# Where the end of an attention layer splits its output weights, and where it turns two projected tiles

## The chip, the cores and the metric

The kernel runs on one core of a Trainium2 chip. A core has a matrix engine (TensorE, PE in the profile, with its weight loads as PEld), a vector engine (VectorE, DVE), an activation engine (ScalarE, ACT), a general one (GpSimd, POOL) and a queue engine (SyncE, SP) that issues most transfers here. Each engine works through its own list of instructions in order and waits on semaphores for the others. The metric is the device time of one execution, in microseconds. Fewer is better.

## The reference

Four layers in a row on one sequence of 2048 tokens of 576 features, each added to its input: attention, a spectral filter, attention again, the filter again, with the same weights both times.

```python
def _A_ref(x, wqkv, wo):            # H = 32 heads of 18, window W = 256
    qkv = (x @ wqkv).reshape(B, S, 3, H, Dh).transpose(2, 0, 3, 1, 4)
    scores = jnp.einsum("bhqd,bhkd->bhqk", q, k) * (Dh ** -0.5)
    mask = (idx[:, None] - idx[None, :] >= 0) & (idx[:, None] - idx[None, :] < W)
    p = _softmax(jnp.where(mask[None, None], scores, -1e9), axis=-1)
    o = jnp.einsum("bhqk,bhkd->bhqd", p, v)
    return (lambda x, *d: x.transpose(*d))(o, 0, 2, 1, 3).reshape(B, S, D) @ wo

def _B_ref(x, w_r, w_i):
    X = jnp.fft.rfft2(x) * (w_r + 1j * w_i)
    return jnp.fft.irfft2(X, s=(S, D), axes=(-2, -1))

x = A_x
x = x + _A_ref(_layernorm(x), A_wqkv, A_wo)
x = x + _B_ref(_layernorm(x), B_w_r, B_w_i)
x = x + _A_ref(_layernorm(x), A_wqkv, A_wo)
x = x + _B_ref(_layernorm(x), B_w_r, B_w_i)
```

## The kernel before

Matrix products are made in two parts for accuracy: an operand is split into a high part, rounded to the matrix engine's format, and a low part, the rest; three products of parts then stand for one. So every weight and every turned tile goes through a copy (high) and a subtraction (low) before PE can use it.

**The attention's rounds.** `layer_a` treats the 32 heads as 8 groups of 4, and a group's 2048 queries as 16 tiles of 128: 128 rounds, numbered 0 to NX - 1 = 127. In a round PE makes the scores `S` of a query tile (`score_max`, L1155), of which DVE takes the row maximum (L1157), ten rounds ahead of their use. It makes the scores again the other way round, `E`, for one key tile against up to three query tiles (`exps`, L1192): 384 wide, but 256 and 128 for the last two tiles of a group (rounds 110 and 111 are such). ACT takes the exponential of each into `P` (L1193), four to a round, POOL masks the finished `P` (L1195, L1198), and PE multiplies `P` with the values into the bank `U` (`part`, L1212). After four query tiles `U` is copied to `us` (L1217), turned (L1226), copied to `ts` and divided (`norm`), and stored to memory as `o_d`. `m_rows` turns the maxima and puts them, as `mt` (L1170), beside the queries.

Up to round MIX - 1 = 117 `bursts` emits this in steps of three scores of each kind: the step's `E` and exponentials, its `S`, then a few `part`s, then the left work such as `norm`, and last, for each round whose fourth exponential lies in the step, `behind(round)`. From round 118 a plain loop emits the exponentials and products that are left, and calls `behind` at the end of each round. There are three PSUM banks for `E`, three for `S`, one (`pj`) for projections and one for `U`.

**What `behind` lays under the rounds.** It prepares the output projection, class `Out`, with OB = NX - 8 = 120. Round 104: `room` issues two transfers on SP's queue, the raw output weights' first two fifths and then the other three (L720), into the tile `ofree`, which the tile of projected inputs has left. Rounds 110, 112, 114, 116 and 118: `split(0)` to `split(4)`, one fifth each, on ACT (L727) and then POOL (L728), from `ofree` into `oroom`. Rounds 107 to 115: `const` loads the next layer's tables, `dc` (L734). Then the loads of inputs and of `o_d`, and `turn` of tiles 0 to 2 in the bank `pj`.

**The end of the attention.** A tile `u` of 128 tokens is projected in eleven pairs of products that need all but the last head group (`early`) and three pairs for that group (`late`), which ends with two sums on DVE into the tile's input (L809). `turn(u, ...)` makes four transposes on PE (L761, L762) into a bank, a copy of the bank to `oT[u % 3]` on ACT or DVE (L766) and a subtraction on DVE (L770). `tail(u)` is two small operations on POOL. The last group's part is turned by `turn_last` (PE, L775) and split by `split_last` (ACT copy L780, DVE subtraction L781). The last round's `us` is turned in `tpz`, whose fourth bank is `U`, and divided straight into `o7` (L1438 to L1442). After these lines `spectral` starts `layer_b`, which projects the tiles 3 to 15 by `unit`, the first thing it asks of PE, in banks that the attention has left.

Of the kernel before, what the change touches and what calls it, by code (L numbers as in the profile page):

```python
# [850 lines left out]
def layer_a(tc, ident, eps, bp, src, dst, wqk_d, wv_d, wo_d, dc_d, gc_d, dram, copy, wvs, second, spectral, share):  # L851

    nc = tc.nc
    V, A, T, P = nc.vector, nc.scalar, nc.tensor, nc.gpsimd
# [14 lines left out]
    if True:  # L869
# [192 lines left out]
        with ExitStack() as c2:  # L1062
# [233 lines left out]
            def bursts():  # L1296
# [8 lines left out]
                for k in range(-(-len(es) // 3)):  # L1305
# [50 lines left out]
                    for x, pair, hp in e:  # L1356
                        if pair == hp == 1:
                            behind(x)
# [7 lines left out]
            OB = NX - 8  # L1366
            out = Out(nc, ident, eps, bp, ov, o7v, srcv, dstv, wo_d, dc_d, gc_d, second)

            def behind(t):
                if copy and t >= 32 and t % 4 == 0 and t < 32 + 16 * len(copy):  # L1370

                    z, r = divmod(t // 4 - 8, 4)
                    P.dma_start(*[a[32 * r:32 * r + 32] for a in copy[z]])
                if t == OB - 16:
                    out.room()
                if 0 <= t - (OB - 10) < 10 and t % 2 == 0:
                    out.split((t - (OB - 10)) // 2)
                if t - OB + 13 in range(0, 10, 2):
                    out.const((t - OB + 13) // 2)
                if t == OB - 3:  # L1380
                    out.filters()
                if t - OB + 8 in range(0, 10, 2):
                    out.load_x(((t - OB + 8) // 2 + 1) % 5)
                if t - OB in (0, 1, 2):
                    out.load_o(t - OB)
                if t == OB + 3:
                    out.last(slice(96, 128), slice(0, 56))
                if t == NX - 2:
                    out.last(slice(0, 64), slice(0, 128))
                if t == NX - 1:  # L1390
                    out.last(slice(64, 96), slice(0, 128))

                if t - OB - 3 in (0, 1, 2, 5):
                    out.tail(min(t - OB - 3, 3))
                if t - OB - 5 in (0, 1, 2):
                    u = t - OB - 5
                    out.turn(u, pp.tile([128, 512], F32, tag="pj", name=f"tpa{u}", bufs=1), V)
                    out.load_o(u + 3)
                if t == NX:

                    A.activation(wp.tile([128, 1], F32, name="se", bufs=1), eps, AF.Sqrt)
# [4 lines left out]
            U = pp.tile([128, 512], F32, tag="U", name="U", bufs=1)  # L1406
# [5 lines left out]
            for t in range(MIX, NX + 2):  # L1412
                loads(t)
                for pair in range(2):
                    for hp in range(2):
                        if t < NX:
                            exps(t, pair, hp)
                    if pair == 0 and t - 2 < NX:
                        pv(t - 2)

                y = t - 3 if t == NX - 2 else t - 4
                if MIX < y < NX - 1 and y % 4 == 3 and t != NX - 1:
                    due.append((norm, *divmod(y // 4, 4)))
                for f, *a in due[:1]:
                    f(*a, *([True] if f is norm else []))
                    due.pop(0)
                behind(t)
            assert not due
            def bank(tag, name):
                return pp.tile([128, 512], F32, tag=tag, name=name, bufs=1 if tag == "pj" else 3)  # L1430
# [12 lines left out]
                             rc.to_broadcast([32, 4, 4, 18]))  # L1443
            out.early(0, None, slice(4, 11))
            out.early(1, [bank("S", f"ops1_{k}") for k in range(2)])
            out.early(2, [bank("E", f"ops2_{k}") for k in range(2)])
            out.tail(4)
            tp = bank("E", "tpl")
            for u in range(4):
                out.turn_last(u, tp[:, 128 * u:128 * u + 128])  # L1450
            for u in range(3):
                out.split_last(u, tp[:, 128 * u:128 * u + 128])
            out.turn(3, U, A)
            out.late(0)
            out.split_last(3, tp[:, 384:512])
            out.late(1)
            out.turn(4, U, A)
            out.late(2)
            out.turn_last(4, tp[:, 0:128])
            out.split_last(4, tp[:, 0:128])  # L1460
# [4 lines left out]
def prompt_kernel(tc, x, wqk, wv, wo, w, dc, fc, gc, ga, m2, out):  # L1465
    nc = tc.nc
    with ExitStack() as ctx, tc.manual_schedule():
        pool = lambda *a, **k: ctx.enter_context(tc.tile_pool(*a, **k))
        dram = pool(name="dram", bufs=1, space=bass.MemoryType.DRAM)
        t = [dram.tile([S, 2 * NF], F32, name=f"x{i}") for i in range(3)]  # L1470
        cr = {k: dram.tile(list(v.shape), F32R, name=k + "r") for k, v in (("dc", dc), ("gc", gc))}
        wvs = dram.tile([2, 128, 5 * D], F32R, name="wvs")
        wo2 = dram.tile([128, 10 * NF], F32, name="wo2")
        drs = [pool(name=f"dram{i}", bufs=1, space=bass.MemoryType.DRAM) for i in range(2)]
        cp, bp = pool(name="ac", bufs=1), pool(name="abig", bufs=1)
        ident = cp.tile([128, 128], F32, name="ident")
        make_identity(nc, ident)
        eps = cp.tile([128, 1], F32, name="eps"); nc.vector.memset(eps, 1e-5)
        layers, share = [], {}
        for i, (s, a, d) in enumerate(((x, t[0], t[1]), (t[1], t[2], out))):  # L1480
            layers.append(layer_a(tc, ident, eps, bp, s, a, wqk, wv, wo2 if i else wo, cr["dc"], cr["gc"], drs[i],
                                  [(cr[k], v) for k, v in (("dc", dc), ("gc", gc))] if i == 0 else None, wvs, i > 0,
                                  lambda *args, i=i, d=d: layer_b(tc, args[0], d, *args[1:], ga, fc, m2, w, wo, wo2, drs[i], layers[1] if i == 0 else None, share), share))
        for layer in layers:
            for _ in layer:
                pass
# [18 lines left out]
```

## Time and profile before

| | us |
|---|---|
| median of 3 runs (1369.69 to 1375.65) | 1369.79 |
| profiled execution, its time | 1370.11 |
| its span | 1368.4 |
| busy in the span: PE / DVE / ACT / POOL | 1337.2 / 901.1 / 780.3 / 644.1 |
| mean granted clock of PE (1 is full) | 0.997 |
| `E` scores L1192 / exponentials L1193, 1024 each | 222.2 / 409.1 |
| projection products L786, the 812 in `ops` banks | 115.4 |
| split's casts L727, 10 / one | 676 ns median |
| split's subtractions L728, 10 / one | 1423 ns median |

The ends of the two attention layers lie near 420 to 482 us and 1122 to 1183 us. A timeline row gives the start in us, the duration (of a merged row: of all its instructions), the engine, the line, the operation and the tiles as out<-in, the count, and in brackets how long the engine had been idle before and what released it. A row of the waits gives who waited for whom, the total in us, the number of times and the longest. A row of stretches gives, from one time to another, the length, the busy us of PE, PEld, DVE, ACT and POOL with their instructions, the granted clock of PE, the share of the DMA engines' time and GB/s.

### The profile page before, as it was taken

To read this page: it belongs to the slowest core of one execution; us is meant where nothing else is said; L and a number is where in the kernel's file an instruction comes from. 1 tells how busy PE (TensorE), PEld (TensorE's weight loads), DVE (VectorE), ACT (ScalarE), POOL (GpSimd) and SP (SyncE) were. 2 spreads that over 40 slices of the span, in tenths; PEclk is the share of its full clock that TensorE was granted. 3 is DMA by queue.
4 is the path that set the end of the run, shared out by engine and by line. 5 is a ranking of instruction groups with operands and counts; after the bars stand their busy time and mean duration, and the time that the engine had idled before them with its cause. 6 is when DMAs were issued, how large, how long until landed. Compare 5 with 4: busy or idle time off the path is not lost.

```text
span 1368.4 us, 33594 instructions
## 1 busy us (share of the span) xinstructions
PE 1337.2 (98%) x11356; PEld 998.4 (73%) x11356; DVE 901.1 (66%) x3060; ACT 780.3 (57%) x1966; POOL 644.1 (47%) x1152
## 2 busy tenths in 40 slices
PE   9999999999999999998999999999999999998998
PEld 8986666666665699975999965566666655898587
DVE  5418777877778376666673157777777785575855
ACT  5622777777778544542355316677777778463223
POOL 2257554555546533476221394445555458112721
PEclk9999999999999999999999999999999999999999
DMA  6756665655446457677873468556555565597874
GB/s 199 209 166 193 205 188 172 186 165 160 151 145 182 127 158 247 222 240 256 271 230 74 113 194 221 163 171 167 153 152 151 160 161 166 143 362 254 287 252 158
DMA packets 202356, 259.11 MB, mean 189 GB/s; under 512 B 104530, under 2 KB 109906, under 8 KB 201674
## 3 DMA queue, kind: packets, MB, share of 16 engines
q1 hardware_dynamic: 191546, 235.76, 57.2%
q10 hardware_dynamic: 7648, 14.96, 3.1%
q0 software_dynamic: 2992, 6.25, 1.8%
q8 instruction: 92, 1.51, 0.5%
q14 instruction: 78, 0.64, 0.2%
HBM read 156.17 MB, written 101.01 MB: 188 GB/s over the span
## 4 chain that ended last, share of the span: by engine, by line
PE 87%; DMA 4%; DVE 3%; ACT 2%; issue 2%; POOL 1%; SPq 0%; ACTq 0%; DVEq 0%; POOLq 0%
PE pj L1098 18%; PE S L1155 12%; PE U L1212 12%; PE vps L991 8%; PE ops L786 7%; PE E L1192 6%; PE po L257 4%; PE pq L512 3%; PE p L491 2%; PE tpo L1226 2%; PE pf L257 2%; PE pi L579 2%; PE pz L295 2%; DMA qs<-mt 1%; PE tpm L1168 1%
## 5 line engine op out<-in xcount | busy, mean ns | idle before, releaser
L1157 DVE CUSTOM_DVE_ANT_0 jk<-S,mask 128x384 bf16<-128x384 f32 (+2 forms) x1024 | 490.6, 529 | 113.1 <-PE E L1192 55.1
L1193 ACT ACTIVATE P<-E 128x384 f32<-128x384 f32 (+2 forms) x1024 | 409.1, 475 | 126.4 <-PE E L1192 98.4
L1195 POOL TENSOR_SCALAR_AFFINE_SELECT P<-P 128x512 f32<-128x512 f32 x256 | 163.2, 637 | 276.4 <-ACT P L1193 257.1
L1155 PE MATMUL S<-ks,qs 63*128 63x384 f32 (+2 forms) x1024 | 270.4, 372 | 1.4 <-DMA qs<-qk_d 0.4
L1192 PE MATMUL E<-qs,ks 64*128 64x384 f32 (+2 forms) x1024 | 222.2, 372 | 5.3 <-DMA qs<-mt 2.5
L1155 PEld LDWEIGHTS S<-ks,qs 63*128 63x128 f32 x1024 | 141.0, 185 | 106.4 <-DVE m L1157 71.9
L1212 PE MATMUL U<-P,vq 128*19 128x128 f32 (+1 forms) x3840 | 188.1, 328 | 0.6
L1098 PE MATMUL pj<-xh,wqh 128*128 128x512 f32 x360 | 156.4, 434 | 1.3 <-DVE sg L1113 0.8
L1212 PEld LDWEIGHTS U<-P,vq 128*19 128x19 f32 x3840 | 95.9, 98 | 77.4 <-issue 24.3
L1198 POOL TENSOR_SCALAR_AFFINE_SELECT P<-P 128x512 f32<-128x512 f32 x224 | 142.9, 638 | 0.0
L1192 PEld LDWEIGHTS E<-qs,ks 64*128 64x128 f32 x1024 | 113.6, 185 | 20.2 <-ACT P L1193 9.3
L1098 PE MATMUL pj<-xh,wql 128*128 128x512 f32 x360 | 124.4, 419 | 0.0
L1098 PE MATMUL pj<-xl,wqh 128*128 128x512 f32 x288 | 122.2, 424 | 0.0
L786 PE MATMUL ops<-oroom 128*128 128x290 f32 (+1 forms) x812 | 115.4, 298 | 0.5 <-DVE ofree L832 0.4
L786 PEld LDWEIGHTS ops<-oroom 128*128 128x128 f32 x812 | 110.3, 189 | 1.3 <-DVE ofree L809 0.7
L1098 PEld LDWEIGHTS pj<-xh,wqh 128*128 128x128 f32 x360 | 67.9, 189 | 32.1 <-issue 10.8
L1157 DVE DVE_READ_ACCUMULATOR2_ANT m<- 128x1 f32 x1024 | 85.1, 83 | 0.0
L1113 DVE TENSOR_TENSOR sg<-pj,sg 128x512 fp32r<-128x512 f32 x72 | 49.5, 687 | 52.0 <-ACT sg L1110 52.0
L1110 ACT CAST sg<-pj 128x512 fp32r<-128x512 f32 x72 | 42.2, 586 | 68.6 <-PE pj L1098 54.8
L1098 PEld LDWEIGHTS pj<-xh,wql 128*128 128x128 f32 x360 | 64.3, 189 | 20.3 <-issue 10.7
L991 PE MATMUL vps<-wvh,xh 128*128 128x288 f32 x320 | 71.4, 304 | 0.3 <-ACT xh L689 0.3
L1098 PEld LDWEIGHTS pj<-xl,wqh 128*128 128x128 f32 x288 | 54.5, 189 | 18.2 <-issue 11.4
(599 smaller groups left out, 2258.6 us busy)
## 6 DMA issues: line engine op xcount, KB each, us to landing
qk_d<-sg SPq DMA_DIRECT2D x56, 512.0 KB
qs<-qk_d SPq DMA_DIRECT2D x384, 72.0 KB
ks<-qk_d SPq DMA_DIRECT2D x348, 72.0 KB
v_d<-vt SPq DMA_DIRECT2D x32, 304.0 KB
vq<-v_d SPq DMA_DIRECT2D x16, 608.0 KB
wt<-in_w SPq DMA_DIRECT2D x16, 580.0 KB
ofree<-x SPq DMA_DIRECT2D x16, 580.0 KB
x<-ofree SPq DMA_DIRECT2D x32, 290.0 KB
```

Source lines behind the costliest of these rows:

```text
L257: T.matmul(ps[:, c, 0:NF], tail[r] if si == 4 else hl_(si), dcs[b // 2][r, b % 2], start=mi == si == 0, stop=si == 4)
L786: self.nc.tensor.matmul(self.ps[u][n][:, 0:self.n], x, self.w[p][:, (2 * wk + n) * self.n:(2 * wk + n + 1) * self.n], start=first and i == ...
L991: T.matmul(ps[:, n, 0:288], xT(xk, c), w[:, wk, n * 288:(n + 1) * 288], start=i == 0, stop=i == len(ks) - 1)
L1098: T.matmul(box["ps"].rearrange("r (n p) -> r n p", n=NT) if second else box["ps"], w[:, wk], x, start=s == 0, stop=s == len(ks) - 1)
L1113: V.tensor_sub(rest[:, 1], by, rest[:, 0].bitcast(F32))
L1155: T.matmul(ps[:, 0:N], q[b:b + 63, pair, i * 128:i * 128 + 128], k[b:b + 63, pair, lo:hi], start=True, stop=True)
L1157: V.tensor_tensor_reduce(out=jk[:, 0:N], in0=ps[:, 0:N], in1=mask[:, 384 - N:384], scale=1.0, scalar=-3e38, op0=ALU.add, op1=ALU.max, accu ...
L1192: T.matmul(ps[:, 0:nq], k[b:b + 64, pair, j * 128:j * 128 + 128], q[b:b + 64, pair, j * 128:j * 128 + nq], start=True, stop=True)
L1193: A.activation(p[:, hl_, 0:nq], ps[:, 0:nq], AF.Exp, scale=SC)
L1195: P.affine_select(out=p[:, :, 0:128], in_=p[:, :, 0:128], pattern=[[0, 4], [1, 128]], compare_op=ALU.is_ge, fill=0.0, base=0, channel_mult ...
L1198: P.affine_select(out=p[:, :, 256:384], in_=p[:, :, 256:384], pattern=[[0, 4], [-1, 128]], compare_op=ALU.is_gt, fill=0.0, base=0, channel ...
L1212: T.matmul(U[32 * h:32 * h + 19, (q0 % 4) * 128:(q0 % 4) * 128 + 128 * (q1 - q0)], vts[n][:, j, h], pt[n, j][:, h, (q0 - j) * 128:(q1 - j) ...
```

## The change

All in `layer_a`, for both attention layers. In `behind` the five splits stand in rounds OB - 12 to OB - 4, which is 108, 110, 112, 114 and 116. At the end, `tail(4)` and `turn(3)` come ahead of `early(2)`, and `turn(4)` stands between `late(0)` and `late(1)`.

```diff
-                if 0 <= t - (OB - 10) < 10 and t % 2 == 0:
-                    out.split((t - (OB - 10)) // 2)
+                if 0 <= t - (OB - 12) < 10 and t % 2 == 0:
+                    out.split((t - (OB - 12)) // 2)
...
             out.early(0, None, slice(4, 11))
             out.early(1, [bank("S", f"ops1_{k}") for k in range(2)])
+            out.tail(4)
+            out.turn(3, U, A)
             out.early(2, [bank("E", f"ops2_{k}") for k in range(2)])
-            out.tail(4)
             tp = bank("E", "tpl")
             for u in range(4):
                 out.turn_last(u, tp[:, 128 * u:128 * u + 128])
             for u in range(3):
                 out.split_last(u, tp[:, 128 * u:128 * u + 128])
-            out.turn(3, U, A)
             out.late(0)
             out.split_last(3, tp[:, 384:512])
+            out.turn(4, U, A)
             out.late(1)
-            out.turn(4, U, A)
             out.late(2)
```

## The prediction

> **What bounds the kernel now.** I read the page's busy shares and its chain of waits, then the timeline of each engine around the ends of both attention layers (420 to 482 us and 1120 to 1190 us), the waits of the DMA queue, and stretches of equal length with their granted clock.
>
> ```profile
> span 1368.4 us, 33594 instructions
> PE 87%; DMA 4%; DVE 3%; ACT 2%; issue 2%; POOL 1%; SPq 0%; ACTq 0%; DVEq 0%; POOLq 0%
> ```
>
> TensorE (PE) carries 87% of the chain, so time in which PE stands still in the attention is added to the end, and work taken from ACT, POOL or DVE counts only where PE waits for it. Only 2% of the chain is ACT's and 1% POOL's, so the question in each part below is whether PE comes to wait for them.
>
> **Part 1, the splits two rounds sooner.** Five `split` steps, in rounds 110 to 118, now stand in rounds 108 to 116. In rounds 110 to 116 a split stands as before; round 108 gains one and round 118 loses one. The gain at 118 first. ACT in layer 1 there:
>
> ```profile
> 447.57 0.66 ACT L727 CAST oroom<-ofree 128x576 fp32r<-128x576 f32 x1
> 448.13 8.75 ACT L1193 ACTIVATE P<-E 128x384 f32<-128x384 f32 x22
> 457.07 1.64 ACT L1193 ACTIVATE P<-E 128x384 f32<-128x384 f32 x4 [0.19 <-PE E L1192]
> ...
> 450.56 0.14 PEld L1212 LDWEIGHTS U<-P,vq 128*19 128x19 f32 x8 [0.24 <-POOL oroom L728]
> ...
> 457.61 0.18 PEld L1192 LDWEIGHTS E<-qs,ks 64*128 64x128 f32 x1 [0.50 <-ACT P L1193]
> ```
>
> The cast occupies ACT 0.56 us (447.57 to 448.13), and 22 exponentials follow without a gap. That looks like a saturated ACT, but at 457.07 ACT has run dry and waits 0.19 us for PE: by then the 0.56 has been repaid whether or not the cast was there. The 0.50 that PE's weight loads wait at 457.61 comes after that, so it is not this cast's. What is left is the 0.24 us wait behind POOL's half of the split, most of it in the shadow of the matmul in flight. I take 0.1 us a layer, between 0 and the whole 0.56.
>
> Now round 108. What a split reads are the raw weights `ofree`, issued by `room` in round 104. Where ACT stands at the end of round 108, and when the weights are there:
>
> ```profile
> 424.47 1.26 ACT L1193 ACTIVATE P<-E 128x384 f32<-128x384 f32 x3 [0.41 <-PE E L1192]
> 425.97 1.15 ACT L1193 ACTIVATE P<-E 128x384 f32<-128x384 f32 x3 [0.24 <-PE E L1192]
> 426.99 0.60 ACT L1217 COPY us<-U 128x512 f32<-128x512 f32 x1
> 427.46 0.98 ACT L1193 ACTIVATE P<-E 128x256 f32<-128x256 f32 x3
> 429.17 0.66 ACT L727 CAST oroom<-ofree 128x576 fp32r<-128x576 f32 x1
> 429.74 0.58 ACT L1193 ACTIVATE P<-E 128x128 f32<-128x128 f32 x3
> ...
> 422.11 0.84 SPq L720 DMA_DIRECT2D ofree<-in_wo  x2
> 429.03 2.36 SPq L734 DMA_DIRECT2D dc<-dcr  x2
> ...
> SPq L734 <- DMA ofree<-in_wo: 3.8, 2, 2.2
> ```
>
> The rounds can be told by width: query tile 110 has only two key tiles ahead of it, so its exponentials are 256 wide (427.46), tile 111's are 128 wide (429.74), and the step with the last of tile 108 is the all-384 group at 424.47; the mixed group at 425.97 (1.15 us, two at 384 and one at 256) is the end of 109 and the start of 110. Hence the moved first split stands between 424.47 + 1.26 = 425.73 and the group of 425.97.
>
> The weights were issued only at 422.11, and SP's queue shows their landing: its next issue, `dc`, waited for them, 2.2 us at the longest, and went at 429.03. The first transfer, with the first two fifths, therefore lands near 429.0. The old place, 429.17, was just behind it. At the new place ACT meets the wait for that landing at 425.73 and, working in order, holds the next exponentials, the copy `us` and the maxima's `mt` behind it; POOL's half of the split holds the masks of tile 109 in the same way. Nothing ahead of 425.73 moves, and the two transfers keep their places on SP's queue, so the landing should stay.
>
> Who waits for ACT:
>
> ```profile
> 426.74 0.82 PE L1192 MATMUL E<-qs,ks 64*128 64x256 f32 x3
> 427.17 0.81 PE L1155 MATMUL S<-ks,qs 63*128 63x384 f32 x2
> 427.91 0.85 PE L1212 MATMUL U<-P,vq 128*19 128x256 f32 x16
> ...
> 1126.99 1.15 ACT L1193 ACTIVATE P<-E 128x384 f32<-128x384 f32 x3 [0.24 <-PE E L1192]
> 1128.93 0.85 PE L1212 MATMUL U<-P,vq 128*19 128x256 f32 x16
> 1130.07 2.46 SPq L734 DMA_DIRECT2D dc<-dcr  x2
> ```
>
> The scores `E` have three banks. PE can fill them once with the group for 425.97; the next, at 426.74, needs a bank that the first held-up exponential frees. From there PE stands, and the maxima of `S` behind it in PE's order leave DVE without work, so neither runs ahead. New times in layer 1: cast at 429.03, exponentials at 429.03 + (429.74 - 429.17) = 429.60, `us` 1.02 later as now, at 430.62, done at 431.22. The `U` products, which read into the bank that `us` empties, now start 0.32 after its end (427.91 against 426.99 + 0.60), behind S products that stretch to 0.81 because DVE is late with their banks. After the pause DVE is not late, and `U` starts between 0 and 0.32 after `us`; I take 0.13, at 431.35. Against 427.91 that is **3.45 us** late. In layer 2 the group starts at 1126.99 now and could start at 1130.07 + 0.57 = 1130.64; `us` ends 1.62 later, `U` at 1132.39 against 1128.93: **3.46 us**. Bounds, a layer: 1.7 (half of it regained, from waits for DVE and ACT that PE has before round 118 and that engines without a backlog would not cause) and 3.7 (nothing regained, even inside the step).
>
> **The clock after the stall.** PE would idle from about 427.0 (the S product issued along with the group of 426.74) to 430.1 (the first exponential, 429.60, and a third of a group's 1.26 to 1.15 us), 3.1 us. What such a pause does to the clock:
>
> ```profile
> 646.41 1.61 PE L257 MATMUL wo<-dc,et 128*128 128x290 f32 x10 [3.06 <-DVE et L251]
> 1263.89 1.20 PE L491 MATMUL p<-ofree,fc 128*64 128x290 f32 x8 [3.23 <-DMA ofree<-yd]
> ...
> 644.48:647.89 3.41, 1.48 (x11) 1.48 (x12) 2.15 (x5) 0.86 (x2) 0.69 (x4) 1.00 0.69 220
> 647.89:651.31 3.42, 3.42 (x14) 3.11 (x14) 0.69 (x1) 1.50 (x3) 0.68 (x4) 0.50 1.04 315
> 1258.88:1262.29 3.41, 1.78 (x16) 1.01 (x11) 2.57 (x4) 0.00 (x0) 1.72 (x3) 1.00 0.36 99
> 1262.29:1265.71 3.42, 1.82 (x11) 1.15 (x12) 0.71 (x2) 0.00 (x0) 0.98 (x2) 1.00 0.91 326
> 1265.71:1269.12 3.41, 3.41 (x21) 2.03 (x21) 2.04 (x5) 0.64 (x1) 1.89 (x3) 1.00 0.90 311
> ...
> 881.59 1.00 PE L1192 MATMUL E<-qs,ks 64*128 64x384 f32 x3
> 883.87 0.62 PE L1192 MATMUL E<-qs,ks 64*128 64x384 f32 x3
> ```
>
> A pause of 3.06 us, most of it in one stretch in which PE was busy 1.48 of 3.41, was followed by a stretch at 0.50 clock. A longer one, 3.23, that fell across the border of two stretches (1.78 and 1.82 busy) was not. So a pause of 3.1 leaves the clock alone only where the border halves it to within about 0.15 us, some one time in ten. After it, a group of three `E` takes 1.00 at half clock (881.59) against 0.62: 38% lost, 1.3 us if PE filled the whole 3.41. The first 1.2 us after the stall are paced by ACT anyway, so I take **1.0 us** a layer, between 0 and 1.3.
>
> [...]
>
> **Part 2, the turns.** The rows of layer 1, and last one of layer 2, which has the same waits:
>
> ```profile
> 470.68 5.92 PEld L786 LDWEIGHTS ops<-oroom 128*128 128x128 f32 x44
> ...
> 470.39 0.45 DVE L1442 TENSOR_TENSOR ofree<-U,rcz 32x288 f32<-32x288 f32 x1
> 477.63 0.19 PEld L786 LDWEIGHTS ops_pj<-oroom 128*128 128x128 f32 x1 [0.16 <-ACT oroom L780]
> 479.96 0.31 PEld L761 LDWEIGHTS U<-ident,ofree 128*128 128x128 f32 x3 [0.65 <-DVE oroom L770]
> 480.35 0.84 PEld L786 LDWEIGHTS ops<-oroom 128*128 128x128 f32 x6
> 481.61 0.56 PEld L786 LDWEIGHTS ops<-oroom 128*128 128x128 f32 x4 [0.34 <-DVE ofree L809]
> ...
> 479.35 0.56 DVE L770 TENSOR_TENSOR oroom<-U,oroom 128x384 fp32r<-128x384 f32 x1 [0.20 <-ACT oroom L766]
> 480.75 0.81 DVE L809 TENSOR_TENSOR ofree<-ofree,ops 128x288 f32<-128x288 f32 x2
> ...
> 1182.70 2.08 DMA x<-ofree
> ```
>
> The same instructions run; four transposes move. `turn(3)` goes ahead of `early(2)`: it needs U free, which DVE's last read of it gives at 470.84, while `early(1)`, the first half of the 44 at 470.68, lasts to about 473.6; so it waits for nothing and its copy and subtraction run on an idle ACT and DVE. It takes 0.39 us of PE (479.96 to 480.35), so all behind it is 0.4 later, and it no longer covers ACT's copy before `late(0)`: PE's wait there grows from 0.16 to about 0.55. `turn(4)`, between `late(0)` and `late(1)`, finds U free: the wait of 0.65 at 479.96 goes. What is late next is DVE. The wait at 481.61 is `unit(3)` asking for banks that `late(1)`'s sums free (480.75 + 0.81 = 481.56). Their place on DVE: 0.4 later by the shift, 0.47 sooner without `turn(3)`'s subtraction (479.35 to the next at 479.82) and 0.2 sooner without its wait for ACT, 0.47 later with `turn(4)`'s ahead of them, less 0.05 of overlap: **+0.15 us** in layer 1, where PE sets the pace behind it. In layer 2 the chain passes through `late(2)`'s sums and the store behind them (1182.70); they lose `turn(4)`'s 0.47 from just ahead of them, 0.15 - 0.47: **-0.3**. Bounds: -0.65 and +0.4 a layer. `tail(4)` moves only on POOL, which is idle there; no DMA moves in this part.
>
> **Sum.** Stall 3.45 + 3.46, clock 2 x 1.0, drain -2 x 0.1, turns +0.15 - 0.3: +8.6 us. The profiled execution took 1370.11 (1.7 of it outside its span); with the change 1378.7. The median of the three runs, 1369.79, is 0.3 lower, so I predict **1378.4 us**.
>
> **The rivals.** *The clock holds* in both layers, because the borders halve the pauses or the pauses are a little short: 1378.4 - 2.0 = 1376.4. For it, the stretch of 1258.88; against it, 647.89. Chance 0.14. *Half is won back*: PE now loses time to DVE and ACT at places such as 427.17, and engines that caught up in the pause would not hold it there: half of 8.6, 1374.1. Against it, the three banks of S and of E let DVE and ACT store at most some 1.2 us of work, and the 0.19 above is already of that kind. Chance 0.16. *Not slower*: the landing is no bar, since SP gets to the weights 3.3 us sooner, at 418.8 instead of 422.11; then ACT meets no wait, PE no pause, and what counts is the drain and the 0.65 at U, at their best 2 x (0.56 + 0.65) less: 1367.4. It decides from the point where the landing precedes 425.73; against it, nothing on SP's queue is changed. Chance 0.04. *Worse*: half clock for more than one stretch, or POOL's masks late too: 1383, chance 0.06.
>
> **How the numbers follow.** The forecast has 0.60, with a range of its own of 1376.5 to 1381 (the clock from 0.2 to 1.3 and the stall to 3.7 a layer). About 0.5%, 6.85 us, is what a measurement of this kernel tells from no change; the border, 1376.64, lies near the rival with the steady clock, of which I count a little under half. Slower: 0.57 + 0.06 + 0.06 = 0.69. Faster: even the fourth case gains only 2.4, so 0.02 is for what I have not seen. Same: 0.29. The range reaches down over the half-regained case and up to the full costs: 1373.0 to 1381.5.
>
> **What would show it.** ACT idle some 3.3 us before the first cast of L727 in each layer, with a DMA of `ofree` as releaser; PE idle about 3.1 us before an `E` group; a stretch at 0.50 clock behind it; the cast gone from 447.57's place; no wait before the transposes into U and a longer one before `unit(3)`. A first cast that starts without a wait, or weights landed before it, would make the prediction wrong.

## The result, and the profile after

The changed kernel takes 1384.9 us (median of 6 runs, 1377.28 to 1386.49); the kernel before, on the same chip, 1369.8 (6 runs, 1368.13 to 1375.65). The ratio is 1.0092, with a 95% interval from 1.0074 to 1.0111: slower by 0.9%. The forecast was 1378.4, within 1373.0 to 1381.5. Direction and place were right, the size was not, and the time lies above the range. The profiled execution took 1386.49, the longest of the six.

The first line of the page of after, and the engines of its chain of waits:

```profile
span 1384.8 us, 33582 instructions
PE 85%; DMA 6%; DVE 3%; issue 2%; ACT 2%; SPq 1%; POOL 1%; DVEq 0%; ACTq 0%; POOLq 0%
```

And the piece of that chain near the end of layer 1's score stage (start, duration, what):

```profile
422.77 6.79 DMA ofree<-in_wo
```

A transfer that the chain of before does not pass at this place (it stays on PE there) is now 6.79 us of the chain: from SP's issue of the raw output weights to the first split. The same place in the timelines of ACT, PE and SP:

```profile
425.07 1.26 ACT L1193 ACTIVATE P<-E 128x384 f32<-128x384 f32 x3 [0.41 <-PE S L1155]
429.58 0.67 ACT L727 CAST oroom<-ofree 128x576 fp32r<-128x576 f32 x1 [3.25 <-DMA ofree<-in_wo]
430.16 1.14 ACT L1193 ACTIVATE P<-E 128x384 f32<-128x384 f32 x3
431.17 0.60 ACT L1217 COPY us<-U 128x512 f32<-128x512 f32 x1
...
427.33 0.44 PE L1155 MATMUL S<-ks,qs 63*128 63x384 f32 x1
430.69 1.23 PE L1192 MATMUL E<-qs,ks 64*128 64x256 f32 x3 [2.93 <-ACT P L1193]
432.18 1.49 PE L1212 MATMUL U<-P,vq 128*19 128x256 f32 x16
...
422.77 0.84 SPq L720 DMA_DIRECT2D ofree<-in_wo  x2
429.64 2.41 SPq L734 DMA_DIRECT2D dc<-dcr  x2
```

ACT waits 3.25 us for the weights, PE waits 2.93 us for ACT, and PE resumes at another speed: the 16 products into `U` take 1.49 us where they took 0.85. The group of exponentials at 424.47 before stands at 425.07 now, so after is 0.60 late when it comes here, and `U` (427.91 before) is 432.18 - 427.91 - 0.60 = 3.67 us later still. The stretches around it:

```profile
426.34:429.75 3.41, 1.43 (x15) 0.74 (x13) 2.22 (x10) 0.17 (x1) 0.58 (x1) 1.00 0.98 355
429.75:433.17 3.42, 2.48 (x17) 1.55 (x21) 1.04 (x4) 2.86 (x8) 2.84 (x4) 0.50 0.58 137
433.17:436.58 3.41, 3.41 (x30) 1.62 (x22) 1.58 (x6) 1.31 (x5) 1.73 (x2) 0.50 0.20 76
436.58:439.99 3.41, 3.41 (x27) 1.74 (x27) 1.73 (x7) 1.56 (x4) 1.26 (x2) 0.50 0.08 10
439.99:443.40 3.41, 3.41 (x41) 1.87 (x41) 3.06 (x13) 3.03 (x8) 2.03 (x3) 1.00 0.86 226
```

Three stretches, 10.24 us, run at a granted clock of 0.50; the forecast had one. PE has 27 products in the last of them and 41 in the next. Layer 2, the timelines again, first one row of before and then those of after:

```profile
1125.49 1.26 ACT L1193 ACTIVATE P<-E 128x384 f32<-128x384 f32 x3 [0.41 <-PE E L1192]
```

```profile
1132.61 1.25 ACT L1193 ACTIVATE P<-E 128x384 f32<-128x384 f32 x3 [0.40 <-PE E L1192]
1136.39 0.67 ACT L727 CAST oroom<-ofree 128x580 fp32r<-128x580 f32 x1 [2.52 <-DMA ofree<-wo]
...
1137.51 1.23 PE L1192 MATMUL E<-qs,ks 64*128 64x256 f32 x3 [2.20 <-ACT P L1193]
1138.99 1.49 PE L1212 MATMUL U<-P,vq 128*19 128x256 f32 x16
```

The stretches of after there:

```profile
1136.31:1139.72 3.41, 2.21 (x13) 1.39 (x17) 0.84 (x3) 3.03 (x8) 2.58 (x4) 0.50 0.82 220
1139.72:1143.14 3.42, 3.42 (x29) 1.53 (x22) 1.78 (x8) 1.31 (x5) 2.00 (x3) 0.50 0.26 79
1143.14:1146.55 3.41, 3.41 (x26) 1.77 (x25) 1.73 (x7) 1.56 (x4) 1.27 (x3) 0.50 0.04 8
```

Again a wait (2.52), a pause (2.20) and three stretches. By how much after is already late when it comes here is 1132.61 - 1125.49 = 7.12, so `U` is later by 1138.99 - 1128.93 - 7.12 = 2.94.

The end of a layer, one row of before in layer 2, then after's weight loads in layer 1 and the matching start in layer 2:

```profile
1171.74 5.98 PEld L786 LDWEIGHTS ops<-oroom 128*128 128x128 f32 x44
...
478.14 2.99 PEld L786 LDWEIGHTS ops<-oroom 128*128 128x128 f32 x22
481.07 0.38 PEld L761 LDWEIGHTS U<-ident,ofree 128*128 128x128 f32 x3
485.53 0.19 PEld L786 LDWEIGHTS ops_pj<-oroom 128*128 128x128 f32 x1 [0.59 <-ACT oroom L780]
486.36 0.38 PEld L761 LDWEIGHTS U<-ident,ofree 128*128 128x128 f32 x3
489.26 3.76 PEld L786 LDWEIGHTS ops<-oroom 128*128 128x128 f32 x28 [0.72 <-DVE ofree L809]
...
1184.87 3.00 PEld L786 LDWEIGHTS ops<-oroom 128*128 128x128 f32 x22
```

The projection's block of 44 (now 22 and 22, with the turn between them) started at 470.68 and starts at 478.14: the score stage of layer 1 costs 478.14 - 470.68 - 0.60 = **6.86 us**. In layer 2 the block moves from 1171.74 to 1184.87: 1184.87 - 1171.74 - 7.12 = **6.01**. Pairing every product with the same product of before gives the same two numbers.

Outside the two score stages the profiled execution loses one larger amount, in the last spectral layer; PE's timeline, and the stretches from there:

```profile
1277.25 2.20 PE L491 MATMUL p<-ofree,fc 128*64 128x290 f32 x8 [3.65 <-DMA ofree<-yd]
```

```profile
1276.26:1279.67 3.41, 2.42 (x9) 1.15 (x10) 0.12 (x1) 0.00 (x0) 0.00 (x0) 0.50 0.94 354
1279.67:1283.08 3.41, 3.41 (x8) 2.22 (x7) 1.31 (x2) 0.00 (x0) 1.36 (x2) 0.50 0.65 252
```

The wait there was 3.23 before, at full clock; now it is 3.65 and two stretches at half clock follow, 3.23 us in all.

### The profile page after: what moved, and what is told of

Its sections match the earlier page's. It is cut to its first block, busy times and chain, and to the rows that moved or that the text cites. A ratio compares the mean times of both kernels' runs of the same rounds, so it can differ in the third digit from the quotient of the medians.

```text
span 1384.8 us, 33582 instructions
## 1 busy us (share of the span) xinstructions
PE 1348.2 (97%) x11356; PEld 1003.1 (72%) x11356; DVE 902.0 (65%) x3060; ACT 780.6 (56%) x1966; POOL 642.7 (46%) x1152
## 4 chain that ended last, share of the span: by engine, by line
PE 85%; DMA 6%; DVE 3%; issue 2%; ACT 2%; SPq 1%; POOL 1%; DVEq 0%; ACTq 0%; POOLq 0%
PE pj L1098 17%; PE S L1155 11%; PE U L1212 11%; PE vps L991 8%; PE ops L786 8%; PE E L1192 6%; PE po L257 4%; PE pq L512 3%; PE p L491 2%; PE pf L257 2%; PE tpo L1226 2%; PE pi L579 2%; PE pz L295 2%; DMA qs<-qk_d 1%; DMA qs<-mt 1%
## 5 line engine op out<-in xcount | busy, mean ns | idle before, releaser
L1192 PE MATMUL E<-qs,ks 64*128 64x384 f32 (+2 forms) x1024 | 225.5, 376 | 10.0 <-ACT P L1193 8.0
L1212 PE MATMUL U<-P,vq 128*19 128x128 f32 (+1 forms) x3840 | 191.5, 333 | 0.6
```

The lines of the kernel that those rows point to most:

```text
L1192: T.matmul(ps[:, 0:nq], k[b:b + 64, pair, j * 128:j * 128 + 128], q[b:b + 64, pair, j * 128:j * 128 + nq], start=True, stop=True)
L1212: T.matmul(U[32 * h:32 * h + 19, (q0 % 4) * 128:(q0 % 4) * 128 + 128 * (q1 - q0)], vts[n][:, j, h], pt[n, j][:, h, (q0 - j) * 128:(q1 - j) ...
```

## The experiments

Theory W is the prediction's: the first of the moved casts waits for weights that land late, ScalarE holds everything behind it, TensorE pauses, and its clock halves. Its rivals: theory T, that the turns cost the time, and theory Q, that the split's work itself does, in rounds without room for it. The table has every run. "Cost" is that of a score stage, in the profiled execution: how much later than before its end is (the products that stood at 470 and 1167 us) less how much later its start was (424 and 1124); added products are left out of the pairing. The pause is TensorE's idle time ahead of its next `E` group; half clock is counted behind the first cast, so the stretch that before too has at 880.00 us is left out.

| run | cast's wait, layers 1, 2 | pause | half clock in the score stages | cost | median, ratio to before (95%) |
|---|---|---|---|---|---|
| the change | 3.25, 2.52 | 2.93, 2.20 | 10.24, 10.24 | 6.86, 6.01 | 1384.9, 1.0092 (1.0074 to 1.0111) |
| e1 splits only | 2.09, 1.72 | 1.76, 1.40 | 6.83, 6.83 | 4.85, 4.54 | 1380.18, 1.0085 (1.0055 to 1.0115) |
| e2 turns only | none | none | none | 0.01, 0.00 | 1372.96, 1.0007 (0.9993 to 1.0021) |
| e3 weights, same order | 3.85, 2.56 | 3.53, 2.23 | 6.83, 6.83 | 6.41, 5.38 | 1380.18, 1.0066 (1.0045 to 1.0087) |
| e4 splits one round sooner | 0.61, 2.01 | none, 1.24 | none, 6.83 | 1.01, 4.58 | 1374.58, 1.0021 (1.0002 to 1.0041) |
| e8 weights first | none | none | none | 0.04, 0.07 | 1370.13, 0.9995 (0.9983 to 1.0008) |
| e6 products, no split moved | none | none | none | 2.92, 2.95 | 1376.46, 1.0036 (1.0018 to 1.0053) |
| e5 products in round 108 | 1.26, 4.04 | none, 0.92 | none, 3.41 | 2.91, 5.56 | 1375.94, 1.0037 (1.0019 to 1.0054) |
| e12 products in round 109 | 1.84, 2.39 | none | none | 2.53, 2.57 | 1375.99, 1.0044 (1.0026 to 1.0061) |
| e7 products in round 110 | 3.17, 3.89 | 2.85, 3.57 | 6.83, 10.24 | 8.14, 10.04 | 1387.35, 1.0109 (1.0086 to 1.0131) |
| e13 products behind the pause | 1.60, 3.03 | 1.27, 2.70 | none, 6.83 | 4.81, 8.92 | 1383.48, 1.0107 (1.0075 to 1.0139) |
| e14 the same, whole change | 1.87, 3.54 | 1.55, 3.21 | 3.41, 6.83 | 6.68, 8.89 | 1382.88, 1.0096 (1.007 to 1.0122) |
| e10 another order of turns | none | none | none | 0.00, 0.62 | 1371.94, 1.0009 (0.9988 to 1.0029) |

The wait differs between executions, since it hangs on when a transfer lands: e1, e7 and e13 are the same program up to that cast, and in layer 1 it waits 2.09, 3.17 and 1.60. All columns but the last are of one execution each, and that is the longest of its runs for e4 and e7 (1381.13, 1393.41) and the shortest for e12 and e13 (1372.93, 1381.62). How far a cost can stray shows in e10's 0.62, in a stage that e10 leaves as it was. The medians of before on these chips were 1371.88 (e1 to e4), 1371.43 (e5 to e8), 1370.56 (e10, e12) and 1370.51 (e13, e14).

**The two parts apart.** e1 has only the first hunk of the diff, e2 only the second.

> The splits in rounds 108 to 116, the turns as before. Theory W (the cast of round 108 waits for weights that have not landed, and PE's pause drops the clock): the first cast of each attention layer waits 2.5 to 3.3 us for the transfer of ofree, half clock for about 10 us behind it, and the median lies 10 to 16 us above before, where the full change lies (+15). Theory T (the turns cost the most of it): within 2 us of before.

> The turns as in the change, the splits as before. Theory W: within 2 us of before, no half clock near 430 or 1135 us, the wait of PE before unit(3) about 0.7 us in place of 0.34, and the net of the stage between -0.3 and +0.2 us a layer. Theory T: 8 us or more above before.

The splits alone carry the loss, the turns none that can be told: T falls, and what is left agrees with W, though e1's casts waited less than the 2.5 to 3.3 us expected. e1's cast and, behind it, its block of 44:

```profile
426.81 0.67 ACT L727 CAST oroom<-ofree 128x576 fp32r<-128x576 f32 x1 [2.09 <-DMA ofree<-in_wo]
...
474.53 5.92 PEld L786 LDWEIGHTS ops<-oroom 128*128 128x128 f32 x44
```

**How the cost grows with the wait.** e4 moves the splits by one round:

```diff
-                if 0 <= t - (OB - 10) < 10 and t % 2 == 0:
-                    out.split((t - (OB - 10)) // 2)
+                if 0 <= t - (OB - 11) < 10 and t % 2 == 1:
+                    out.split((t - (OB - 11)) // 2)
```

> The splits one round sooner only (109 to 117), the turns as before. Theory W: the first cast comes about 1.9 us later than in round 108 and waits 1.0 to 1.5 us in each layer; PE pauses about as long; if the clock drops only behind pauses of about 3 us, the median is 2 to 3.5 us above before. If a pause of 1.3 us drops it too, 8 us or more. Theory Q: as much as in round 108, 8 us or more.

Layer 1, with a wait of 0.61, no single pause of PE and no half clock, loses 1.01; layer 2, with 2.01 and two stretches, 4.58. e4's median is 2.7 us above before, as expected for short pauses, but its two layers differ, and the 1.24 us pause of layer 2 did drop the clock. Over the eight score stages of the change, e1, e3 and e4 the cost fits the wait and about 1.3 us for each stretch of 3.41 at half clock, within 0.5 us: e1's layer 1 is 2.09 + 2 x 1.3 = 4.69 (4.85 measured), the change's layer 1 is 3.25 + 3 x 1.3 = 7.15 (6.86).

**Weights sooner.** Two tries, both with the whole change; e3 puts `room` in round 103, e8 in 102:

```diff
-                if t == OB - 16:
+                if t == OB - 18:
                     out.room()
```

> The full change, and room() one round sooner (103), so that SP issues the raw weights ahead of the twelve loads of queries and keys of round 104. Theory W: the weights land some 5 us sooner, the first cast waits for nothing, PE has no pause, the clock stays at 1.00 there, and the median is within 2 us of before. Theory Q (it is the work of a split in round 108 that is in the way, its cast on ACT and its subtraction on POOL, wherever the weights are): the cost stays, 8 us or more above before.

This missed by its own making: SP's order did not change. Round 103 ends in the step of three scores in which round 104 begins, and the twelve loads that round 104 asks for stand at the head of that step, so on SP's queue the weights are still behind `ks`:

```profile
417.29 2.33 SPq L1130 DMA_DIRECT2D ks<-qk_d  x6
419.72 0.84 SPq L720 DMA_DIRECT2D ofree<-in_wo  x2
```

So it is in effect a second measurement of the change itself: waits of 3.85 and 2.56, costs of 6.41 and 5.38.

> The whole change, but the output weights' DMAs are issued two rounds sooner too, in round 102, a step ahead of the twelve loads of round 104. Theory W (the first split's casts wait for weights that land late; ScalarE, held in order behind them, starves TensorE, and the clock halves behind the pause): the weights land near 420 us, the first cast waits under 0.3 us in both layers, the stretches at half clock near 430 and 1136 us are gone, and the time comes to within 2 us a layer of before, 1368 to 1374 us. Rival Q (it is the split's own work, moved to rounds where ScalarE and VectorE have none to spare, that costs): no wait on a DMA, but still 8 us or more of the loss, 1380 us or more. A third way: the twelve loads of round 104, now behind the weights, come late, and a wait for ks or qs appears in rounds 104 to 107 of 1 us or more.

Here the order did change. SP's and ACT's timelines and the weight loads of e8:

```profile
416.82 0.83 SPq L720 DMA_DIRECT2D ofree<-in_wo  x2
418.25 2.29 SPq L1130 DMA_DIRECT2D qs<-qk_d  x6
420.78 4.74 SPq L1130 DMA_DIRECT2D ks<-qk_d  x6
...
425.04 1.25 ACT L1193 ACTIVATE P<-E 128x384 f32<-128x384 f32 x3 [0.40 <-PE E L1192]
426.17 0.68 ACT L727 CAST oroom<-ofree 128x576 fp32r<-128x576 f32 x1
...
471.28 2.99 PEld L786 LDWEIGHTS ops<-oroom 128*128 128x128 f32 x22
```

The cast follows the exponentials without a wait, and the block starts at 471.28: 0.60 after before, and e8 already was 0.57 late at 425.04 (424.47 before). All the rest of the change is in this kernel, and it takes what before took. Nor did a wait for `ks` or `qs` take its place: the score stages cost 0.04 and 0.07. So Q falls, and W's first half is shown: it is the wait for the weights. These two costs also show that the splits win nothing at the drain, since they stand where the change put them.

**Keeping PE busy.** If the wait costs only because PE stands still, other work for PE in that place should cover it. Twelve products of 128x128 by 128x512 (128*128 in the trace), whose result nothing uses, are added to the kernel before (e6) and to the one with the early splits alone (e5, e12):

```diff
+                if t == OB - 12:
+                    hp = pp.tile([128, 512], F32, tag="pj", name="heat", bufs=1)
+                    for _ in range(12):
+                        T.matmul(hp, qs[0][:, 0, 0:128], ks_[0][:, 0, 0:512], start=True, stop=True)
```

> The kernel before with the same twelve products in round 108: what they cost where there is no wait to fill. About 12 x 0.24 = 2.9 us a layer, 5.8 us in all, at full clock: 1375 to 1378 us. So if the kernel with the early splits and these products is no more than 2 us above this one, the products cover the wait.

> Only the splits two rounds sooner (turns as before), and twelve more products of 128x128 by 128x512 in round 108, whose result nothing uses: TensorE has work while ScalarE waits for the weights. If the half clock comes from TensorE's own pause: the cast still waits 1.7 to 3.3 us for the DMA, the granted clock stays at 1.00 from 425 to 440 us and from 1130 to 1145 us, each layer is longer by 3.5 to 4.2 us than before, and the time is 6 to 8.5 us above before. If the half clock has another cause (the split's work, the DMA): the stretches at 0.50 stay, and each layer is longer by 6 us or more.

> Only the splits two rounds sooner, with the twelve products of 128x128 by 128x512 in round 109: right behind TensorE's pause, a round sooner than in the run that had ten of them in round 110. The splits alone had two stretches at half clock in each score stage, though TensorE was busy all through the first of them. If what keeps the clock down is how little of the array the score stage's products use, full products there end it after one stretch of 3.41 us: each layer longer than before by the wait (1.7 to 2.1), the products (2.9) and 1.3, so 6 us. If it is not: two stretches or three again, and the products themselves at half clock: 8 to 10 us a layer, 1386 us or more.

e12 (OB - 11 for OB - 12) was meant to follow the pause, but its products fell just into it, which makes it the cleanest of the three. Its PE and ACT timelines:

```profile
424.44 3.01 PE L1381 MATMUL heat<-ks,qs 128*128 128x512 f32 x12
427.38 0.44 PE L1155 MATMUL S<-ks,qs 63*128 63x384 f32 x1
427.38 0.56 PE L1192 MATMUL E<-qs,ks 64*128 64x256 f32 x3
...
425.27 0.67 ACT L727 CAST oroom<-ofree 128x576 fp32r<-128x576 f32 x1 [1.84 <-DMA ofree<-in_wo]
```

ACT waits 1.84 and 2.39 us for the weights, PE waits for nothing, and the granted clock stays at 1.00 (417.50 to 434.50; its mean over the span is 0.997, as in before). The score stages cost 2.53 and 2.57, less than the 2.92 and 2.95 that the products cost alone. So these waits of ACT's cost nothing while PE had work, and the half clock came with PE's pause, not from the transfer or the split. The medians agree: with the products, the early splits cost nothing that can be told (e5 1375.94, e6 1376.46, on the same chip), and the kernels with useless work added have ratios of 1.0037 (e5) and 1.0044 (e12) against 1.0085 without (e1); the intervals of e5 and e1 do not meet, those of e12 and e1 just do. In e5 layer 1 agrees (2.91 at a wait of 1.26); in layer 2 the wait of 4.04 outlasts the products, which leaves a pause of 0.92, and that is enough for one stretch at half clock. Its row in PE's timeline, and the stretches around it:

```profile
1134.36 1.09 PE L1192 MATMUL E<-qs,ks 64*128 64x256 f32 x3 [0.92 <-ACT P L1193]
```

```profile
1131.79:1135.20 3.41, 2.49 (x20) 1.35 (x20) 2.00 (x8) 1.96 (x5) 1.21 (x1) 1.00 0.81 231
1135.20:1138.61 3.41, 3.41 (x30) 1.62 (x31) 1.50 (x5) 2.15 (x9) 2.14 (x5) 0.50 0.44 130
1138.61:1142.03 3.42, 3.42 (x41) 1.85 (x40) 2.82 (x14) 1.93 (x7) 2.53 (x3) 1.00 0.02 4
```

**Why two or three stretches.** The same products behind the pause ask whether the half clock lasts because the score stage's products fill little of the array (63*128, 64*128 and 128*19 in the trace, against 128*128). e7 has ten of them in round 110; e13 and e14 have twelve behind the first `E` group after the pause, e14 with the whole change:

```diff
                     for f in e:
                         exps(*f)
+                    if k == 147:
+                        hp = pp.tile([128, 512], F32, tag="pj", name="heat", bufs=1)
+                        for _ in range(12):
+                            T.matmul(hp, qs[0][:, 0, 0:128], ks_[0][:, 0, 0:512], start=True, stop=True)
```

> Only the splits two rounds sooner, with ten of these products in round 110, behind the pause. If the length of the half clock depends on how full TensorE's array is behind the pause: one or two stretches of 3.41 us, where the splits alone had two and the whole change three. If it doesn't: two or three, and the time is that of the splits alone (1380) and 2 x 10 x 0.24 = 4.8 us, or more where the products fall into the half clock: 1385 to 1390 us.

> Only the splits two rounds sooner, with the twelve products of 128x128 by 128x512 behind the first three E products after TensorE's pause, so that they fill the first stretch at half clock and not the pause; their result is not used. Open is why the half clock lasts two or three stretches of 3.41 us in the score stage. Theory F (the score stage's products, 63 or 64 rows and 19 columns of the array, count for too little): filled with full products the first stretch ends it, one stretch of 3.41 us in each layer; the layers are longer than before by the wait, 1.3 for the stretch and 2.9 to 4.0 for the products. Rival (the length has nothing to do with how full the array is): two or three stretches in each layer, and the products at half clock, some 5 us of them.

> The whole change with the same twelve products at the same place, as a second pair of layers for the same question. Theory F: one stretch of 3.41 us in each score stage, where the whole change had three. Rival: two or three again.

No clear answer. Layer 1 of e14 had one stretch, as theory F (that the score stage's products count for too little) has it; e13's had none, so it says nothing of the length; in both layers 2, and in both of e7, there were two or three. The stretches of e13's layer 2, where the twelve products began at 1134.21 and lasted to 1139.70:

```profile
1132.82:1136.23 3.41, 3.18 (x8) 2.48 (x9) 0.00 (x0) 2.14 (x7) 3.04 (x4) 0.50 0.71 196
1136.23:1139.65 3.42, 3.42 (x11) 2.19 (x9) 0.00 (x0) 0.00 (x0) 0.00 (x0) 0.50 0.04 13
```

PE was busy 3.18 of the first, 2.02 of it with full products, and a second followed; in e5 above a stretch of score products alone was enough to end it. Only in layer 1 of e14 did PE work through the whole first stretch; in the other four it stood for a part (busy 1.32 to 3.18 of 3.41), so F was tried as it was meant only once. What sets the number of stretches stays open. F is neither shown nor refuted.

**Another order of the turns.** e10 leaves the splits as before, puts `turn(3)` ahead of `early(2)`, and parts `turn(4)`: its four transposes stand right behind the last tiles' own, and its copy and subtraction behind `late(1)`.

```diff
+            out.turn(3, U, A)
             out.early(2, [bank("E", f"ops2_{k}") for k in range(2)])
...
+            out.turn_pe(4, U)
...
             out.late(1)
-            out.turn(4, U, A)
+            out.turn_split(4, U)
```

> The splits as before (rounds 110 to 118); of the end of a layer another order: the fourth tile's turn ahead of the second's first products, and the fifth tile's four transposes right behind that, with their copy and subtraction left behind late(1), so that TensorE has the second's first products while ScalarE copies. Before, ScalarE's or VectorE's part was awaited 0.65 us at the turn and 0.34 us at the fourth tile. By my reading of these rows 0.4 to 0.6 us a layer is won in the trace, 0.8 to 1.2 us in all, 1369 us: too little for the ratio to show. If the waits only move to other products: within 0.2 us a layer of before.

In the trace the end of each layer is 0.32 us shorter at `unit(3)`, a little under the 0.4 to 0.6 expected, and the ratio can't tell it. No version was measurably faster than the kernel before.

## Why the prediction was right or wrong

- **The landing** was put near 429.0, from SP's queue. The first cast starts at 429.58, which is 428.98 without the 0.60 by which after is late there. Right. That it is the cause, e8 shows: the rival in which the weights land in time had SP reach them at 418.8; with SP there at 416.82 the loss is gone. Its further gain, 1367.4, did not come.
- **The stall**, 3.45 (431.35 - 427.91 is 3.44) and 3.46 until `U`: measured 3.67 and 2.94. The chain through ACT to PE's banks was as read, a pause of 2.93 and 2.20 against 3.1. The size moves with the landing (2.09 in e1, 3.85 in e3).
- **The clock**, 2 x 1.0, with 0 to 1.3 as its bounds: the step that failed. What the score stages cost beyond the stall is 6.86 - 3.67 = 3.19 and 6.01 - 2.94 = 3.07. Over three stretches that is 1.06 and 1.02 each, so the price of a stretch was right; the number of stretches was the mistake, one taken from the row of 647.89 where three came. That row stands in another stage, and nothing in the profile of before showed a half clock behind a pause in this place (its one half-clock stretch in a score stage, at 880.00 behind a pause of 2.03, stands alone too). Nor is one stretch the rule at that row's own place, which no version touches: near 650 us the fourteen profiles have no half clock in four (e2, e8, e12, e14), one stretch in five and two in five (e3 to e7). "Half clock for more than one stretch" stood among the rivals at 0.06; its 1383 was the nearest number. The two terms are too small by 2.2 and 2.1, which with the other steps here (-0.3 for the stall, +0.2 for the drain, +0.1 for the turns) makes 4.2 of the 6.5 us by which the forecast fell short.
- **The drain**, -0.1 a layer: nothing. The cast left its place, but the exponentials run dry all the same, as ACT's rows of after show, and e8's block keeps its lag of 0.60:

```profile
455.02 1.69 ACT L1193 ACTIVATE P<-E 128x384 f32<-128x384 f32 x4
456.89 0.87 ACT L1193 ACTIVATE P<-E 128x384 f32<-128x384 f32 x2 [0.17 <-PE E L1192]
457.95 6.38 ACT L1193 ACTIVATE P<-E 128x384 f32<-128x384 f32 x16 [0.19 <-PE E L1192]
```

- **The turns**, +0.15 and -0.3: in layer 1 +0.19 at `unit(3)` and +0.09 from the next block of loads on, with the three waits as forecast: that before `late(0)` 0.59 (forecast 0.55, 0.16 before), none at 486.36 (0.65 before), and 0.72 before `unit(3)` (0.34 before). Layer 2 shows +0.19 at `unit(3)` too and -0.19 from two blocks later on; but there e1, with the turns of before, shows -0.16, and e2, with the turns alone, -0.27, so the gain that is theirs is some 0.1 at most.
- **The rest** of the 6.5 us, some 2.3, is not assigned; and the amounts above are of the profiled execution, 1.6 us longer than the median. The profiled execution's 3.23 in the last spectral layer is a candidate but no effect of the change that was shown: half clock in that layer stands in e8 (1262.53) and e10 (1263.86) too, where nothing waits for the weights, and not in before, e1, e2, e3 or e6. How much half clock there is differs between executions of the change: as their times rise from 1377.28 to 1386.49, the mean granted clock falls from 0.994 to 0.987 without an exception, which by estimate (twice the missing share of the span) is some 17 to 36 us at half clock in all.

## What to carry to other kernels

Work that is moved ahead must have its operands there: follow them back to the queue that issues them, and move the issue past what stands in front of it, in the step order in which it is really emitted (e3 moved it by a round and the order stayed). A wait on an in-order engine that feeds the matrix engine cost nothing here while the matrix engine had other work (1.84 and 2.39 us in e12). When it had none, it cost about its own length, and in this kernel's score stage another 1.3 us for each stretch of half clock behind it (both by the fit over eight score stages). When a pause is priced, count those stretches as an unknown, here from none to three, and not as the one that another stage showed.

## What the hardware showed that was not expected

A pause of 0.92 us (e5, layer 2) was followed by a stretch at half clock, and a wait of ACT of 0.61 without a pause (e4, layer 1) was not. Behind pauses of 1.24 to 3.57 us the score stage ran 0, 3.41, 6.83 or 10.24 us at half clock, always one to three whole stretches of 3.41 or none, with no plain tie to the pause: 3.53 brought two (e3), 2.20 three (the change), 1.27 none (e13). Nor does PE's busy share of a stretch decide alone: in the change two stretches with PE busy all 3.41 us (433.17 and 436.58) stand at 0.50, one followed by another at 0.50, the other by one at 1.00.

Across different products it decides still less: 2.49 us busy, nearly all with the score stage's products, were followed by half clock in e5 (1131.79), and 1.78 busy with spectral products of 128 rows (128*64 in the trace) by full clock in before (1258.88). Two stretches with nearly the same pause and the same busy time, first e4's in layer 2 (pause 1.24, score stage products alone, half clock followed) and then e13's in layer 1 (pause 1.27, products of 128*128 behind it, full clock followed):

```profile
1131.79:1135.20 3.41, 2.51 (x24) 1.22 (x24) 2.66 (x12) 1.40 (x4) 1.22 (x2) 1.00 0.91 310
426.26:429.67 3.41, 2.55 (x10) 1.88 (x11) 0.38 (x2) 2.77 (x8) 2.91 (x4) 1.00 0.84 205
```

This pair agrees with theory F, but no run was built to test what a stretch needs to keep the clock, and it stays open. So does the way back: of the half-clock stretches of the score stage that PE filled, five behind the moved split were followed by another (the change at 433.17 and 1139.72, e1 at 428.90 and 1132.05, e3 at 1134.60), while the change's at 436.58 and 1143.14 and e5's at 1135.20 were followed by full clock. The change's three stretches are, in each layer, one that still holds the end of the pause (busy 2.48 and 2.21), one of those five, and a last one.
